# A spectral-filter and SwiGLU block: filter rows at -k turned round through DRAM, first loads reordered, nine normalisations on GpSimd

## Chip, core and metric

The kernel runs on one core of a Trainium2 chip. The metric is the device time of one execution in microseconds (us). Three runs of the kernel before gave 253.07, 253.15 and 253.79 us; their median is 253.15 us. A profile is one more execution, recorded by the hardware profiler. Its instructions span 252.6 us from the first to the last, and the execution took 254.42 us, so 1.82 us lie outside the span.

## What is computed

```
mod = (silu(c) @ w_mod).reshape(1, 6, 1, 640)
sa, ca, ga, sb, cb, gb = (mod[:, i] for i in range(6))
h = layernorm(x) * (1 + ca) + sa                       # x: 1 x 2048 x 640, bf16
y = irfft2(rfft2(h) * (w_r + 1j * w_i))                # the spectral filter
x = x + ga * y
h = layernorm(x) * (1 + cb) + sb
out = x + gb * ((silu(h @ w_gate) * (h @ w_up)) @ w_down)   # 640 -> 1728 -> 640
```

The filter `w_r`, `w_i` has 2048 rows (one for each frequency along the tokens) of 321 bf16 values (642 bytes). The kernel uses that the transform of a real signal holds a frequency k and its mirror -k together, so beside filter row k it needs row -k.

## The kernel before

**The order of the work is written out by hand.** Every engine runs its instructions in the order of the program text, with no scheduler in between. TensorE (PE), VectorE (DVE), ScalarE (ACT) and GpSimd (POOL) each have one such queue. SyncE (SP) does nothing but issue transfers, also in order. An engine that comes to a waiting instruction holds up all that stands behind it.

**The front stage** (L264 to L488) is what the change is about. The tokens are cut into eight steps `t` of two 128-token tiles each (tiles T = 2t and 2t+1):

- `bn` (L343) takes mean and variance of a tile on DVE; `bn_act` (L348) does it on ACT for the tiles in `BA` = (1, 3, 5, 11). `rstd_of` (L352) makes 1/sqrt(variance + eps), with its power on POOL (L361). `normed` (L363) writes the two normalised tiles, on DVE (L366), into one of three buffer pairs `XN`.
- `tok(t)` (L369) multiplies them by a token table `Gtab` (ten matmuls, L377) into PSUM banks 0 to 2, and ACT copies the result to `YS` (L380).
- `ddft(t)` (L382) multiplies that by `Rs`, the channel table scaled by 1 + ca (24 matmuls, L322 and L325), into PSUM banks 3 to 6, and ACT copies the result to `A_sb` (L393). For the last step, DVE and ACT share this copy (L397).
- `Rs` needs 1 + ca, which comes from `mod_cols` (L317), matmuls with the part `wm_ca` of `w_mod`. `idle_pe` (L305) are matmuls whose result nobody uses.
- `sa_cols`, `sa_rows` and `sa_fix` bring in `sa` the same way, in steps 5, 7 and after.

**The loads** (L264 to L290) stand at the top: the first two pairs of x tiles, `wm_ca`, then the rest of x between pieces of `Gtab` and the channel table `Rp`, the `sa` part of `w_mod`, a table `Ktab`, the filter rows at +k (`load_w`, L278: 128 partitions x 8 rows for each of `w_i`, `w_r`, into the slots 0 to 7 of `Wt[:, 0]` and `Wt[:, 2]`), and the first further part of `w_mod`, `wm_r[0]` (L290), which the filter stage reads at L638.

**The filter rows at -k** go to the slots 8 to 15 of the same tiles. Partition s of slot 8 + m needs row 256 m + 256 - s, and partition 0 needs row 256 m + 128. `gather` (L333) fetches one slot by an indirect load on POOL, with the row of each partition taken from `ridx`. There are 16 such loads (L336), handed out between POOL's other work by `fetch`.

**The filter stage** (L490 to L719) starts with `wsum` (L328, L331), which adds the parts of `Wt`: the columns 48 to 63 on DVE, the others on POOL. It reads all 16 slots of both, +k and -k. `prod` (L574) then multiplies the filter into the transformed data, group by group of four columns, and PE transposes and multiplies back (L551, L581, L621). `ga_mod` (L641, matmuls L638) stands on PE between the first two groups and reads `wm_r[0]` and `sc_rep`. Before, `sc_rep` is written on POOL at L669, after the front. Four transposing transfers (`t2_dma`, L502) bring the later groups, and three loads stand behind them on SP (L510 to L513).

**After that** come the inverse transform and the residual (L1152 to L1210), and the feed-forward part in four chunks (L1211 on). The change touches neither.

Of the kernel before, what the change touches and what calls it, by code (L numbers as in the profile page):

```python
# [10 lines left out]
F32 = mybir.dt.float32  # L11
# [21 lines left out]
def xslot(T):  # L33
    return NS * (T % 2) + T // 2
# [139 lines left out]
def adaln_block_kernel(ctx, tc, A_x, A_w_r, A_w_i, B_x, B_w_gate, B_w_up, B_w_down, c, w_mod, out):  # L174
# [52 lines left out]
    ridx = const.tile([P, 1], I32, name="ridx")  # L227
# [38 lines left out]
    nc.sync.dma_start(xh_sb[:, :, 0:1, :], x_v[:, :, 0:1, :])  # L266
    nc.sync.dma_start(xh_sb[:, :, 1:2, :], x_v[:, :, 1:2, :])
    nc.sync.dma_start(wm_ca[:, 0:3], wmca_v[:, 0:3])
    nc.scalar.dma_start(Rp[:, 4:5], R_dram[:, 4:5])
    nc.sync.dma_start(wm_ca[:, 3:5], wmca_v[:, 3:5])  # L270
    Gd = G_dram.rearrange("p t k f -> p t (k f)")
    nc.scalar.dma_start(Gtab[:, 0:2], Gd[:, 0:2])
    def load_x(xl, xh, gl, gh):
        nc.sync.dma_start(xh_sb[:, :, xl:xh, :], x_v[:, :, xl:xh, :])
        nc.sync.dma_start(Gtab[:, gl:gh], Gd[:, gl:gh])

    def load_w(i, w):
        nc.sync.dma_start(Wt[:, i, 0:8, 0:321], w.rearrange("(k s) l -> s k l", s=256)[0:P])  # L278

    load_x(2, 3, 2, 6)  # L280
    nc.sync.dma_start(Rp[:, 0:4], R_dram[:, 0:4])
    load_x(3, 4, 6, 8)
    load_x(4, 6, 8, 12)
    load_x(6, 8, 12, 16)
    nc.sync.dma_start(wm_sa[:], wm_v[:, :, 0:D])
    nc.sync.dma_start(Ktab[:], K_dram)
    load_w(0, A_w_i)
    load_w(2, A_w_r)
    wm_m = wm_v[:, :, 2 * D:6 * D].rearrange("p k (i d) -> p k i d", i=4)
    nc.sync.dma_start(wm_r[:, :, 0, :], wm_m[:, :, 0, :])  # L290
# [42 lines left out]
    def gather(k):  # L333
        i, m = 2 * (k // NS), k % NS
        w = (A_w_i, A_w_r)[k // NS]
        nc.gpsimd.indirect_dma_start(Wt[:, i, NS + m, 0:321], None, w, bass.IndirectOffsetOnAxis(ap=ridx[:, 0:1], axis=0),  # L336
                                     element_offset=256 * m * 321)

    if True:
        CS = (4, 0, 1, 2, 3)  # L340
        BA = (1, 3, 5, 11)

        def bn(T):  # L343
            for k in range(2):
                nc.vector.bn_stats(bn6a[:, k, :], x_sb[:, xslot(T), 320 * k:320 * k + 320])
            nc.vector.bn_aggr(mv[:, T, :], bn6a[:])
# [5 lines left out]
        def rstd_of(t):  # L352
            ts = slice(2 * t, 2 * t + 2)
            if 2 * t + 1 in BA:
                u = slice(2 * t + 1, 2 * t + 2)
                nc.vector.scalar_tensor_tensor(vtmp[:, u], mv[:, u, 0], mv[:, 2 * t + 1, 0:1], st1[:, u], ALU.mult, ALU.subtract)
                nc.vector.tensor_scalar(vtmp[:, u], vtmp[:, u], -1.0, EPS, ALU.mult, ALU.add)
                nc.vector.tensor_scalar_add(vtmp[:, 2 * t:2 * t + 1], mv[:, 2 * t, 1:2], EPS)
            else:
                nc.vector.tensor_scalar_add(vtmp[:, ts], mv[:, ts, 1], EPS)  # L360
            nc.gpsimd.tensor_tensor(rstd[:, ts], vtmp[:, ts], mhalf[:, 0:2], ALU.pow)  # L361

        def normed(t):  # L363
            for h in range(2):
                T = 2 * t + h
                nc.vector.tensor_scalar(XN[t % 3][h][:], x_sb[:, xslot(T), :], mv[:, T, 0:1], rstd[:, T:T + 1],  # L366
                                        ALU.subtract, ALU.mult)

        def tok(t, mid=()):  # L369
            Y = banks(0, 3, [6, 256])  # L370
            for s, c5 in enumerate(CS):
                if s == 3 and mid:
                    mid.pop(0)()
                for h in range(2):
                    xn = XN[t % 3][h]
                    lhsT = xn[:, 0:512].rearrange("p (m r) -> p r m", r=4)[:, c5, :] if c5 < 4 else xn[:, 512:640]
                    nc.tensor.matmul(Y[:, s, :], lhsT=lhsT, rhs=Gtab[:, 2 * t + h, :], start=(h == 0 and s % 2 == 0),  # L377
                                     stop=(h == 1 and (s % 2 == 1 or s == 4)), skip_group_check=True)
            Ys = YS[t % 3]
            nc.scalar.copy(Ys[:], Y[:, 0:5])  # L380

        def ddft(t, mid=()):  # L382
            Ys = YS[t % 3]
            for ck in range(2):
                dft_d(banks(3 + 2 * ck, 2, [4, 256]), [Ys[:, CS.index(c5), 128 * ck:128 * ck + 128] for c5 in range(NC5)])
                if mid:
                    mid.pop(0)()
            for m in mid:
                m()
            Av = A_sb[:, :, t].rearrange("p l k c r -> p k c l r")  # L390
            av = banks(3, 4, [8, 256])[:, :, 0:RC].rearrange("p (k r) (c l) -> p k c l r", k=2, c=2)
            if t < NS - 1:
                nc.scalar.copy(Av, av)  # L393
            else:
                for ls in (slice(48, 64), slice(0, 48), slice(64, 81)):
                    for ck, cp in ((0, nc.vector.tensor_copy), (1, nc.scalar.copy)):
                        cp(Av[:, ck, :, ls], av[:, ck, :, ls])  # L397

        cps = psum[:, 7, 500:500 + NC5]
# [7 lines left out]
        gathers = list(range(2 * NS))  # L407

        def fetch(n):
            for _ in range(min(n, len(gathers))):  # L410
                gather(gathers.pop(0))
# [8 lines left out]
        fetch(1)  # L420
        normed(0)
        idle_pe(4)
        mps = psum[:, 7, 0:32 * NC5]
# [9 lines left out]
        tok(0)
        for r in (1, 3):
            nc.scalar.mul(Rs[:, 0, r, :], Rp[:, r, :], one_p_ca[:, r:r + 1])
        normed(1)
        for r in range(2, 4):
            nc.gpsimd.tensor_scalar(Rs[:, 1, r, :], Rp[:, 4, :], m4c[:, r:r + 1], 1.0, ALU.mult, ALU.mult)
        for r in range(2):
            nc.vector.tensor_scalar_mul(Rs[:, 1, r, :], Rp[:, 4, :], m4c[:, r:r + 1])  # L440
        for r in (0, 2):
            nc.vector.tensor_scalar_mul(Rs[:, 0, r, :], Rp[:, r, :], one_p_ca[:, r:r + 1])
        bn(4)
        fetch(1)
        rstd_of(2)
        fetch(2)
        bn(6)
        normed(2)
        idle_pe(2)

        def sa_cols():
            mps = psum[:, 7, 431:431 + NC5]
            mod_cols(mps, wm_sa)
            nc.vector.tensor_copy(sa_col[:], mps)
            nc.gpsimd.tensor_scalar_mul(sa4[:], mask4[:], sa_col[:, 4:5])
            nc.gpsimd.tensor_copy(_rev(SL, 0, [[257, 4], [132, 2], [16, NS]]),
                                  sa_col[:, 0:4].unsqueeze(2).unsqueeze(3).to_broadcast([P, 4, 2, NS]))
            nc.gpsimd.tensor_copy(_rev(SL, 1024, [[1, 4], [132, 2], [16, NS]]),
                                  sa4[:].unsqueeze(2).unsqueeze(3).to_broadcast([P, 4, 2, NS]))

        def sa_rows():
            sps = psum[:, 7, 431:431 + NL]
            for i in range(10):
                r, c2 = i // 2, i % 2
                nc.tensor.matmul(sps, lhsT=SL[:, r, c2, :], rhs=Rp[:, r, 81 * c2:81 * c2 + 81], start=(i == 0), stop=(i == 9))
            nc.vector.tensor_scalar_mul(SAb[:], sps, 256.0)

        def sa_fix():
            fps = psum[:, 7, 431:431 + NL]
            nc.tensor.matmul(fps, lhsT=TF, rhs=SAb[:], start=True, stop=True)  # L470
            nc.vector.tensor_copy(FSA[:], fps)

        for t in range(1, NS):
            tok(t)
            if t < 6:
                (bn_act if 2 * t + 5 in BA else bn)(2 * t + 5)
                rstd_of(t + 2)
                if t < 5:
                    bn(2 * t + 6)
                normed(t + 2)  # L480
                fetch(1 + t % 2)
            ddft(t - 1)
            if t == 5:
# [11 lines left out]
    if True:  # L495
# [173 lines left out]
        nc.gpsimd.tensor_copy(sc_rep[:], sc_f[:].unsqueeze(2).to_broadcast([P, NC5, 128]))  # L669
# [640 lines left out]
```

## Time and profile before

| | us |
|---|---|
| median of three runs | 253.15 |
| the profiled execution | 254.42 |
| its span | 252.6 |
| PE busy in the span | 238.8 (95%) |
| DVE, ACT, POOL busy | 202.3, 171.1, 76.5 |
| ACT's last three copies of the front stage (L397) | 37.91 to 38.73 |
| first `wsum` on DVE starts (L331) | 39.97 |

The page of a profile has busy times by engine, the span in 40 slices of 6.3 us with a digit for the busy tenths, the transfers by queue (q1 is SP's, q10 ACT's, q0 POOL's), and the chain of work that ended last. In a line of the chain stand the start, the time and the engine with its source line. A timeline line has start, duration, engine, line, operation, output <- input and shape. `L331` is line 331 of the kernel before. A wait "for DMA" ends when a transfer has landed.

### The profile page before, as it was taken

The page shows a single profiled execution, that of the slowest core. Times are in us where ns is not written, and L with a number is a line of the kernel's source. Part 1 is how long each engine was busy: PE and PEld are TensorE (multiplying, and loading weights), DVE is VectorE, ACT ScalarE, POOL GpSimd, SP SyncE. Part 2 cuts the span into 40 slices and gives each one's busy share as a digit, 9 for nine tenths or more (in the row PEclk, how much of TensorE's full clock was granted, in tenths as well). Part 3 has the DMA queues.
Part 4 walks back from the last instruction along what each step waited for, and adds up shares of the span by engine and source line. Part 5 has one row for each costly group of instructions (what it writes and reads, how often), then busy time and mean ns, then how long its engine had stood idle before and what let it go on. Part 6 is the DMA issues. An engine that isn't in the chain of part 4 may idle for free.

```text
span 252.6 us, 5944 instructions
## 1 busy us (share of the span) xinstructions
PE 238.8 (95%) x2240; PEld 186.5 (74%) x2240; DVE 202.3 (80%) x493; ACT 171.1 (68%) x327; POOL 76.5 (30%) x111
## 2 busy tenths in 40 slices
PE   7587887999999999999999999999999999999994
PEld 2366866899989888778887778888675666656773
DVE  3695827997669999698998996778998788779964
ACT  5379876898689788858965387876247777774220
POOL 6675788671060633102001320000442000003410
PEclk9689999999999999999999999999999999999999
DMA  7999418998899999910001420300511000000111
GB/s 179 370 380 327 150 42 155 150 346 307 252 302 298 349 277 229 207 33 4 0 3 36 84 61 31 56 0 4 104 52 55 0 0 0 4 0 1 55 52 52
DMA packets 41310, 31.61 MB, mean 125 GB/s; under 512 B 22017, under 2 KB 37954, under 8 KB 41154
## 3 DMA queue, kind: packets, MB, share of 16 engines
q1 hardware_dynamic: 38704, 25.45, 36.9%
q0 software_dynamic: 2144, 5.58, 8.9%
q10 hardware_dynamic: 434, 0.21, 0.5%
q8 instruction: 17, 0.28, 0.5%
q14 instruction: 11, 0.09, 0.1%
HBM read 23.91 MB, written 2.62 MB: 105 GB/s over the span
## 4 chain that ended last, share of the span: by engine, by line
PE 83%; ACT 5%; DMA 3%; POOL 3%; DVE 2%; issue 2%; SPq 1%; DVEq 0%; ACTq 0%
PE psum L1031 35%; PE psum L902 19%; PE psum L1001 6%; PE psum L879 3%; DMA rM<-in_w_mod_dram 3%; PE psum L653 3%; PE psum L581 3%; PE psum L551 2%; PE psum L1172 2%; PE psum L1175 2%; PE psum L989 2%; POOL rW L336 2%; PE psum L377 1%; ACT rY L584 1%; PE psum L621 1%
## 5 line engine op out<-in xcount | busy, mean ns | idle before, releaser
L1031 PEld LDWEIGHTS <-rW 128*128 128x128 bf16 (+1 forms) x429 | 42.0, 98 | 12.6
L1031 PE MATMUL psum<-rW 128*128 128x256 bf16 (+1 forms) x247 | 42.2, 287 | 0.0
L928 POOL TENSOR_TENSOR rM<-rM,rL 128x320 f32<-128x320 f32 x6 | 5.4, 907 | 96.6 <-ACT rL L927 96.6
L902 PEld LDWEIGHTS <-rE 128*128 128x128 f16 (+1 forms) x196 | 19.0, 97 | 7.8
L902 PE MATMUL psum<-rE 128*128 128x320 f16 (+1 forms) x147 | 22.9, 299 | 0.0
L574 DVE TENSOR_TENSOR rM<-psum,rW 128x384 bf16<-128x384 f32 (+2 forms) x42 | 20.6, 547 | 2.1 <-PE psum L551 1.4
L1069 ACT COPY rX<-psum 128x384 f32<-128x384 f32 (+2 forms) x27 | 14.0, 519 | 7.3 <-PE psum L1031 7.2
L1062 ACT COPY rH<-psum 128x384 f32<-128x384 f32 (+2 forms) x27 | 13.9, 517 | 7.3 <-PE psum L1031 6.5
L1031 PEld LDWEIGHTS <-rE 128*128 128x128 f16 x156 | 15.2, 98 | 4.8
L1066 DVE TENSOR_TENSOR rH<-psum,rM 128x512 bf16<-128x512 f32 (+1 forms) x24 | 15.0, 624 | 4.4 <-PE psum L1031 2.6
L1085 ACT ACTIVATE rL<-psum 128x384 bf16<-128x384 f32 (+2 forms) x27 | 14.4, 532 | 5.4 <-PE psum L1031 3.4
L1070 DVE TENSOR_TENSOR rX<-psum,rX 128x384 f32<-128x384 f32 (+2 forms) x27 | 16.3, 604 | 1.7 <-ACT rX L1069 1.4
L1056 ACT COPY rM<-psum 128x384 f32<-128x384 f32 (+2 forms) x27 | 13.9, 515 | 4.0 <-PE psum L1031 3.9
L1031 PE MATMUL psum<-rE,rY 128*128 128x256 f16 (+1 forms) x78 | 15.6, 290 | 0.0
L1031 PE MATMUL psum<-rW,rE 128*128 128x256 bf16 (+1 forms) x78 | 15.6, 290 | 0.0
L1177 DVE SCALAR_TENSOR_TENSOR rM<-psum,rX 128x640 f32<-128x640 f32 x16 | 13.1, 821 | 2.7 <-ACT rL L657 1.4
L1086 ACT ACTIVATE rL<-rX 128x384 bf16<-128x384 f32 (+2 forms) x27 | 15.1, 558 | 0.0
L584 ACT CAST rY<-psum 128x512 bf16<-128x512 f32 (+2 forms) x21 | 11.8, 574 | 4.1 <-PE psum L581 3.7
L1001 PE MATMUL psum<-rW 128*128 128x256 bf16 x130 | 14.5, 273 | 0.0
L871 DVE TENSOR_TENSOR rA<-psum,rM 128x320 bf16<-128x320 f32 (+1 forms) x27 | 12.1, 472 | 2.4 <-PE psum L879 2.3
L1001 PEld LDWEIGHTS <-rW 128*128 128x128 bf16 x130 | 12.7, 98 | 1.6 <-issue 0.2
L1074 DVE TENSOR_TENSOR rH<-psum,rH 128x384 bf16<-128x384 f32 (+1 forms) x21 | 12.9, 615 | 0.0
(213 smaller groups left out, 641.7 us busy)
## 6 DMA issues: line engine op xcount, KB each, us to landing
out_dram<-rA SPq DMA_DIRECT2D x31, 80.0 KB
rM<-in_w_mod_dram SPq DMA_DIRECT2D x3, 800.0 KB
rA<-in_B_w_down_dram SPq DMA_DIRECT2D x2, 960.0 KB
rY<-in_B_w_gate_dram POOLq DMA_DIRECT2D x2, 832.0 KB
rM<-in_w_mod_dram SPq DMA_DIRECT2D x1, 1600.0 KB
rX<-in_A_x_dram SPq DMA_DIRECT2D x4, 320.0 KB
rX<-in_A_x_dram SPq DMA_DIRECT2D x2, 640.0 KB
rW<-in_B_w_gate_dram SPq DMA_DIRECT2D x2, 640.0 KB
```

Of the source, the lines that this page charges most:

```text
L574: nc.vector.tensor_tensor(PP[:, :, hl], xv[:, :, hl], in1, ALU.mult)
L584: nc.scalar.copy(Y2[:, 0:n, :], yps[:, 0:n, :])
L902: nc.tensor.matmul(o, lhsT=lhs[rows(k), k], rhs=rhs[rows(k), k], start=start and k == ks[0], stop=stop and k == ks[-1], skip_group_check=True)
L1001: nc.tensor.matmul(gu[u], lhsT=Wgu[:, u, c5, ff * 128:(ff + 1) * 128], rhs=h2T[:, :, c5, :], start=(c5 == 0), stop=(c5 == NC5 - 1))
L1031: nc.tensor.matmul(o[:, f], lhsT=w, rhs=b, start=(start and f == 0 and i == 0), stop=(stop and f == len(groups[g]) - 1 and i == len(ops) - ...
L1056: nc.scalar.copy(c0, X)
L1062: nc.scalar.copy(c2, X)
L1066: nc.vector.tensor_tensor(c11, Z, c0, ALU.add)
L1069: nc.scalar.copy(c3, X)
L1070: nc.vector.tensor_tensor(c22, Y, c3, ALU.add)
L1085: nc.scalar.activation(g21, X, ACT.Silu, scale=-1.0)
L1086: nc.scalar.activation(g22, c22, ACT.Silu, scale=-1.0)
```

## The change

The 16 indirect loads and their index `ridx` go. In their place POOL issues two transfers from DRAM to DRAM (`flip`), each of which writes 8 x 127 rows of one filter, in reversed order, to a scratch tensor. SP then loads each scratch tensor to partitions 1 to 127 (`unflip`), after a wait for its flip, and partition 0 is loaded by `edge`.

```
+    Wflip = [dram.tile([P, NS, 321], BF16, name=n) for n in ("wflip_i", "wflip_r")]
+    def edge(i, w):
+        nc.sync.dma_start(Wt[0:1, i, 8:16, 0:321], w.rearrange("(k s) l -> s k l", s=256)[P:P + 1])
+    def flip(w, f):
+        ncol = w.ap[0][0]
+        nc.gpsimd.dma_start(f[1:P].rearrange("p k l -> k p l"),
+                            bass.AP(tensor=w.tensor, offset=w.offset + 255 * ncol, ap=[[256 * ncol, NS], [-ncol, P - 1], [1, 321]]))
+    def unflip(i, f):
+        nc.sync.dma_start(Wt[1:P, i, 8:16, 0:321], f[1:P])
...
-    def gather(k):
-        i, m = 2 * (k // NS), k % NS
-        w = (A_w_i, A_w_r)[k // NS]
-        nc.gpsimd.indirect_dma_start(Wt[:, i, NS + m, 0:321], None, w, bass.IndirectOffsetOnAxis(ap=ridx[:, 0:1], axis=0),
-                                     element_offset=256 * m * 321)
```

In the built program the source of an `unflip` is 1016 rows of 321 values in one run, and its destination 127 partitions x 8 rows. A `flip` has 8 x 127 rows on both sides. An `edge` has 8 rows.

The loads on SP now stand in this order: x for steps 0 to 3 and `Gtab` for steps 0 and 1, both parts of `wm_ca`, `Rp`, the rest of `Gtab` and x in turns, the `sa` part, the filter rows at +k, the two edges, `Ktab`, then the two unflips, and `wm_r[0]` behind them. The transposing transfers follow as before.

```
+        nc.gpsimd.memset(SL[:], 0.0)
+        nc.gpsimd.tensor_copy(sc_rep[:], sc_f[:].unsqueeze(2).to_broadcast([P, NC5, 128]))
+        bn(0)
+        rstd_of(0, 0)
+        bn_act(1)
...
+        tok(0)
+        rstd_of(1)
+        bn(4)
+        normed(1)
+        rstd_of(2)
+        flip(A_w_i, Wflip[0])
+        flip(A_w_r, Wflip[1])
+        for i in range(2):
+            unflip(2 * i, Wflip[i])
+        nc.sync.dma_start(wm_r[:, :, 0, :], wm_m[:, :, 0, :])
+        tok(1)
...
+        BA = (1, 3, 5)
+        NP = {2: (0,), 3: (0,), 4: (0, 1), 5: (0, 1), 6: (0, 1), 7: (0,)}
+        def shift(t):
+            ts = slice(2 * t, 2 * t + 2)
+            nc.vector.scalar_tensor_tensor(nb1[:, ts], mv[:, ts, 0], -1.0, rstd[:, ts], ALU.mult, ALU.mult)
+        def normed_pool(t, hs):
+            for h in hs:
+                T = 2 * t + h
+                nc.gpsimd.tensor_scalar(XN[t % 3][h][:], x_sb[:, xslot(T), :], rstd[:, T:T + 1], nb1[:, T:T + 1],
+                                        ALU.mult, ALU.add)
```

`tok(0)` and `tok(1)` now stand ahead of `mod_cols` on PE, so that x and the tables are needed first and `wm_ca` later. Of the 16 normalised tiles, nine are written by POOL (the list `NP` holds 1 + 1 + 2 + 2 + 2 + 1) instead of DVE; DVE makes their offset by `shift`. Tile 11 moves from `bn_act` on ACT to `bn` on DVE. `ddft` uses PSUM banks 4 to 7 (banks 0 to 3 for its last step), and `mod_cols` bank 3. The last `YS` copy is shared by DVE and ACT. `sc_rep` is written at the start. From `t2_pe` on, the text differs only in the PSUM banks that `t2_pe` uses.

More of the change, by code (lines that the diff above doesn't have):

```diff
@@ L226, in adaln_block_kernel @@
     m4c = const.tile([P, 4], F32, name="m4c")
-    ridx = const.tile([P, 1], I32, name="ridx")
+    nb1 = const.tile([P, NT], F32, name="nb1")
     sa4 = const.tile([P, 4], F32, name="sa4")
@@ L265, in adaln_block_kernel, with load_x, load_g @@
     wmca_v = wm_v[:, :, D:2 * D]
[L266 to L270, printed above, removed]
     Gd = G_dram.rearrange("p t k f -> p t (k f)")
-    nc.scalar.dma_start(Gtab[:, 0:2], Gd[:, 0:2])
-    def load_x(xl, xh, gl, gh):
+    dram = ctx.enter_context(tc.tile_pool(name="dram", bufs=1, space=bass.MemoryType.DRAM))
+    Wflip = [dram.tile([P, NS, 321], BF16, name=n) for n in ("wflip_i", "wflip_r")]
+    def load_x(xl, xh):
         nc.sync.dma_start(xh_sb[:, :, xl:xh, :], x_v[:, :, xl:xh, :])
+    def load_g(gl, gh):
         nc.sync.dma_start(Gtab[:, gl:gh], Gd[:, gl:gh])
@@ L278, in load_w @@
         nc.sync.dma_start(Wt[:, i, 0:8, 0:321], w.rearrange("(k s) l -> s k l", s=256)[0:P])
[L280 to L284, printed above, removed]
+    def edge(i, w):
[6 more added lines that the diff above has]
+        nc.sync.dma_start(Wt[1:P, i, 8:16, 0:321], f[1:P])
+    load_x(0, 1)
+    load_x(1, 2)
+    nc.scalar.dma_start(Gtab[:, 0:2], Gd[:, 0:2])
+    load_x(2, 3)
+    load_g(2, 4)
+    load_x(3, 4)
+    nc.sync.dma_start(wm_ca[:, 0:3], wmca_v[:, 0:3])
+    nc.sync.dma_start(wm_ca[:, 3:5], wmca_v[:, 3:5])
+    nc.sync.dma_start(Rp[:], R_dram)
+    load_g(4, 8)
+    load_x(4, 6)
+    load_g(8, 12)
+    load_x(6, 8)
+    load_g(12, 16)
     nc.sync.dma_start(wm_sa[:], wm_v[:, :, 0:D])
-    nc.sync.dma_start(Ktab[:], K_dram)
     load_w(0, A_w_i)
     load_w(2, A_w_r)
+    edge(0, A_w_i)
+    edge(2, A_w_r)
+    nc.sync.dma_start(Ktab[:], K_dram)
     wm_m = wm_v[:, :, 2 * D:6 * D].rearrange("p k (i d) -> p k i d", i=4)
-    nc.sync.dma_start(wm_r[:, :, 0, :], wm_m[:, :, 0, :])
     nc.vector.memset(ones[:], 1.0)
@@ L298, in adaln_block_kernel, with idle_pe @@
                             pattern=[[-1, 128]], channel_multiplier=1)
-    nc.gpsimd.iota(ridx[:], pattern=[[0, 1]], base=256, channel_multiplier=-1)
-    nc.gpsimd.memset(ridx[0:1], 128)
     nc.scalar.activation(warm[:], warm[:], ACT.Silu)
-    def idle_pe(n, w=4):
+    def idle_pe(n, w=4, b=5):
         for i in range(n):
-            nc.tensor.matmul(banks(5, 1, [128 * w]), lhsT=ones[:], rhs=ones[:].unsqueeze(1).to_broadcast([P, w, 128]),
+            nc.tensor.matmul(banks(b, 1, [128 * w]), lhsT=ones[:], rhs=ones[:].unsqueeze(1).to_broadcast([P, w, 128]),
                              start=True, stop=True)
@@ L331, in wsum, with bn @@
         eng.tensor_tensor(v[1], v[2], v[0], ALU.add)
-    def gather(k):
-        i, m = 2 * (k // NS), k % NS
-        w = (A_w_i, A_w_r)[k // NS]
-        nc.gpsimd.indirect_dma_start(Wt[:, i, NS + m, 0:321], None, w, bass.IndirectOffsetOnAxis(ap=ridx[:, 0:1], axis=0),
-                                     element_offset=256 * m * 321)
     if True:
         CS = (4, 0, 1, 2, 3)
-        BA = (1, 3, 5, 11)
-        def bn(T):
-            for k in range(2):
+        BA = (1, 3, 5)
+        NP = {2: (0,), 3: (0,), 4: (0, 1), 5: (0, 1), 6: (0, 1), 7: (0,)}
+        def bn(T, stats=True, aggr=True):
+            for k in range(2 * stats):
                 nc.vector.bn_stats(bn6a[:, k, :], x_sb[:, xslot(T), 320 * k:320 * k + 320])
-            nc.vector.bn_aggr(mv[:, T, :], bn6a[:])
+            if aggr:
+                nc.vector.bn_aggr(mv[:, T, :], bn6a[:])
         def bn_act(T):
@@ L350, in bn_act, with rstd_of, normed @@
             nc.scalar.activation(junk1[:], x_sb[:, xslot(T), :], ACT.Identity, scale=1.0 / D, accum_out=mv[:, T, 0:1])
-        def rstd_of(t):
+        def rstd_of(t, one=None):
             ts = slice(2 * t, 2 * t + 2)
-            if 2 * t + 1 in BA:
-                u = slice(2 * t + 1, 2 * t + 2)
+            a, u = slice(2 * t, 2 * t + 1), slice(2 * t + 1, 2 * t + 2)
+            if one == 0:
+                ts = a
+            elif one == 1:
+                ts = u
+            if one != 0 and 2 * t + 1 in BA:
                 nc.vector.scalar_tensor_tensor(vtmp[:, u], mv[:, u, 0], mv[:, 2 * t + 1, 0:1], st1[:, u], ALU.mult, ALU.subtract)
                 nc.vector.tensor_scalar(vtmp[:, u], vtmp[:, u], -1.0, EPS, ALU.mult, ALU.add)
-                nc.vector.tensor_scalar_add(vtmp[:, 2 * t:2 * t + 1], mv[:, 2 * t, 1:2], EPS)
+                if one is None:
+                    nc.vector.tensor_scalar_add(vtmp[:, a], mv[:, a, 1], EPS)
             else:
                 nc.vector.tensor_scalar_add(vtmp[:, ts], mv[:, ts, 1], EPS)
-            nc.gpsimd.tensor_tensor(rstd[:, ts], vtmp[:, ts], mhalf[:, 0:2], ALU.pow)
-        def normed(t):
-            for h in range(2):
+            nc.gpsimd.tensor_tensor(rstd[:, ts], vtmp[:, ts], mhalf[:, 0:ts.stop - ts.start], ALU.pow)
+        def normed(t, hs=range(2)):
+            for h in hs:
                 T = 2 * t + h
@@ L367, in normed, with tok @@
                                         ALU.subtract, ALU.mult)
-        def tok(t, mid=()):
+        def shift(t):
+            ts = slice(2 * t, 2 * t + 2)
+            nc.vector.scalar_tensor_tensor(nb1[:, ts], mv[:, ts, 0], -1.0, rstd[:, ts], ALU.mult, ALU.mult)
+        def normed_pool(t, hs):
+            for h in hs:
+                T = 2 * t + h
+                nc.gpsimd.tensor_scalar(XN[t % 3][h][:], x_sb[:, xslot(T), :], rstd[:, T:T + 1], nb1[:, T:T + 1],
+                                        ALU.mult, ALU.add)
+        def tok(t):
             Y = banks(0, 3, [6, 256])
             for s, c5 in enumerate(CS):
-                if s == 3 and mid:
-                    mid.pop(0)()
                 for h in range(2):
@@ L378, in tok, with ddft @@
                                      stop=(h == 1 and (s % 2 == 1 or s == 4)), skip_group_check=True)
+            if t < NS - 1:
+                nc.scalar.copy(YS[t % 3][:], Y[:, 0:5])
+            else:
+                nc.vector.tensor_copy(YS[t % 3][:, 0:3], Y[:, 0:3])
+                nc.scalar.copy(YS[t % 3][:, 3:5], Y[:, 3:5])
+        def ddft(t):
             Ys = YS[t % 3]
-            nc.scalar.copy(Ys[:], Y[:, 0:5])
-        def ddft(t, mid=()):
-            Ys = YS[t % 3]
+            zb = [banks(4 + 2 * ck, 2, [4, 256]) for ck in range(2)]
+            if t == NS - 1:
+                zb = [banks(0, 2, [4, 256]), banks(2, 2, [4, 256])]
             for ck in range(2):
[L385 to L389, printed above, removed]
+                dft_d(zb[ck], [Ys[:, CS.index(c5), 128 * ck:128 * ck + 128] for c5 in range(NC5)])
             Av = A_sb[:, :, t].rearrange("p l k c r -> p k c l r")
-            av = banks(3, 4, [8, 256])[:, :, 0:RC].rearrange("p (k r) (c l) -> p k c l r", k=2, c=2)
             if t < NS - 1:
[L393 to L399, printed above, removed]
+                nc.scalar.copy(Av, banks(4, 4, [8, 256])[:, :, 0:RC].rearrange("p (k r) (c l) -> p k c l r", k=2, c=2))
+                return
+            for ls in (slice(48, 64), slice(0, 48), slice(64, 81)):
+                for ck, cp in ((0, nc.vector.tensor_copy), (1, nc.scalar.copy)):
+                    cp(Av[:, ck, :, ls], zb[ck][:, :, 0:RC].rearrange("p r (c l) -> p c l r", c=2)[:, :, ls])
+        cps = psum[:, 3, 500:500 + NC5]
         for k in range(NC5):
@@ L406, in adaln_block_kernel @@
                                 op=ALU.add)
[L407 to L411, printed above, removed]
         nc.gpsimd.memset(SL[:], 0.0)
-        fetch(2)
+        nc.gpsimd.tensor_copy(sc_rep[:], sc_f[:].unsqueeze(2).to_broadcast([P, NC5, 128]))
         bn(0)
+        rstd_of(0, 0)
         bn_act(1)
-        rstd_of(0)
-        bn(2)
-        bn_act(3)
[L420 to L423, printed above, removed]
+        bn(2, True, False)
+        rstd_of(0, 1)
+        normed(0, (0,))
+        bn(2, False, True)
+        normed(0, (1,))
+        bn_act(3)
+        bn_act(5)
+        idle_pe(6)
+        tok(0)
[9 more added lines that the diff above has]
+        tok(1)
+        idle_pe(2)
+        bn(6)
+        bn(7)
+        shift(2)
+        normed(2, [1])
+        normed_pool(2, (0,))
+        mps = psum[:, 3, 0:32 * NC5]
         mod_cols(mps, wm_ca, range(0, 3), 32)
@@ L426, in adaln_block_kernel @@
         mod_cols(mps, wm_ca, range(3, 5), 32)
-        idle_pe(3)
+        idle_pe(2)
         mps = mps.rearrange("p (c w) -> p c w", w=32)[:, :, 0]
-        rstd_of(1)
+        rstd_of(3)
         nc.vector.tensor_scalar_add(one_p_ca[:], mps, 1.0)
-        bn_act(5)
         nc.vector.tensor_scalar_mul(m4c[:], mask4[:], one_p_ca[:, 4:5])
[L433 to L439, printed above, removed]
-            nc.vector.tensor_scalar_mul(Rs[:, 1, r, :], Rp[:, 4, :], m4c[:, r:r + 1])
[L441 to L449, printed above, removed]
+        for r in range(4):
+            nc.vector.tensor_scalar_mul(Rs[:, 1, r, :], Rp[:, 4, :], m4c[:, r:r + 1])
+            if r < 2:
+                nc.vector.tensor_scalar_mul(Rs[:, 0, r, :], Rp[:, r, :], one_p_ca[:, r:r + 1])
+            else:
+                nc.scalar.mul(Rs[:, 0, r, :], Rp[:, r, :], one_p_ca[:, r:r + 1])
         def sa_cols():
-            mps = psum[:, 7, 431:431 + NC5]
+            mps = psum[:, 3, 431:431 + NC5]
             mod_cols(mps, wm_sa)
@@ L461, in sa_rows @@
         def sa_rows():
-            sps = psum[:, 7, 431:431 + NL]
+            sps = psum[:, 3, 431:431 + NL]
             for i in range(10):
@@ L468, in sa_fix @@
         def sa_fix():
-            fps = psum[:, 7, 431:431 + NL]
+            fps = psum[:, 3, 431:431 + NL]
             nc.tensor.matmul(fps, lhsT=TF, rhs=SAb[:], start=True, stop=True)
             nc.vector.tensor_copy(FSA[:], fps)
-        for t in range(1, NS):
+        for t in range(2, NS):
             tok(t)
+            if t == 2:
+                ddft(0)
+            if t < 7:
+                if t + 1 in NP:
+                    shift(t + 1)
+                normed(t + 1, [h for h in range(2) if h not in NP.get(t + 1, ())])
+                normed_pool(t + 1, NP.get(t + 1, ()))
+            for T in (2 * t + 4, 2 * t + 5):
+                if T < NT:
+                    bn(T)
             if t < 6:
-                (bn_act if 2 * t + 5 in BA else bn)(2 * t + 5)
                 rstd_of(t + 2)
[L478 to L483, printed above, removed]
+            if t == 6:
                 sa_cols()
-                fetch(16)
             if t == 7:
                 sa_rows()
-        ddft(7, [sa_fix])
+            ddft(t - 1)
+        sa_fix()
+        ddft(7)
     Em = rE.cut(0, [64, 128])
@@ L523, in t2_pe @@
             n = len(ls)
-            tp = banks((0, 1, 6, 7)[slot], 1, [8, 128], BF16)
+            tp = banks(4 + slot, 1, [8, 128], BF16)
             for i, l in enumerate(ls):
@@ L668, in adaln_block_kernel @@
         nc.gpsimd.memset(rY.cut(4096, [1600])[:], 0.0)
-        nc.gpsimd.tensor_copy(sc_rep[:], sc_f[:].unsqueeze(2).to_broadcast([P, NC5, 128]))
         t2_pe(0)
```

## The prediction

> **What bounds the kernel now.** I read the page first. PE is busy for 95% of the span and holds 83% of the chain that ended last, but the change lies in the first 40 us, so I asked for the chain, the timeline and the transfers there.
>
> ```profile
> 26.02 1.01 POOL rW L336
> 27.34 0.96 POOL rW L336
> 28.31 0.75 POOL rstd L361
> 29.08 0.81 DVE rE L366 x2
> ...
> 32.13 1.17 POOL rW L336
> 33.60 0.96 POOL rW L336
> ```
>
> This is the chain between 20 and 42 us. The reader is to see that the indirect loads stand on it: POOL computes rstd for a step only after the loads queued ahead of it, and DVE's normalisation waits. What the front hands over to is the timeline at 40 us:
>
> ```profile
> 39.97 0.43 DVE L331 TENSOR_TENSOR rW<-rW 128x512 bf16<-128x512 bf16 x1 [0.29 <-issue]
> 40.32 0.16 DVE L519 TENSOR_TENSOR rM<-psum,FSA 128x4 bf16<-128x4 f32 x1
> 40.39 0.55 DVE L331 TENSOR_TENSOR rW<-rW 128x512 bf16<-128x512 bf16 x1
> 40.54 0.32 PE L551 MATMUL psum<-Ktab,rM 128*128 128x192 bf16 x2 [0.40 <-DVE rM L519]
> 40.54 0.10 PEld L551 LDWEIGHTS <-rM 128*128 128x128 bf16 x1 [0.55 <-issue]
> 40.62 0.58 PEld L638 LDWEIGHTS <-sc_rep 128*128 128x128 bf16 x5
> 40.70 0.84 PE L638 MATMUL psum<-rM,sc_rep 128*128 128x320 bf16 x5
> ```
>
> The first wsum (L331) starts at 39.97 and waits for no transfer: every filter row is there. From its start to the end of the span are 252.6 - 39.97 = 212.6 us of work that the change leaves alone. **So the question is when wsum can start in the changed kernel**: when the front ends, or when the filter rows at -k land, whichever is later.
>
> **The rows at -k.** Removed are 16 indirect loads of 1.05 us (16.8 us of POOL) and two index instructions (0.2 us). Each had 128 rows of 642 bytes and took 2.6 to 6.2 us from issue to landing, median 4.4. Added are two flips, two edges and two unflips. An unflip moves 1016 rows of 642 bytes. What a row costs is read where the +k rows (the same shape) are loaded, at 22 to 23 us. The columns are packets, MB and the share of 16 engines' time:
>
> ```profile
> q1 hardware_dynamic: 470, 0.30, 104.8%
> ```
>
> 16 engines x 1 us x 1.048 / 470 packets = 35.7 ns for a row on one engine (over 22 to 24 us it is 37.1). I take 36. An unflip is then 1016 x 36 ns = 36.6 us of one engine's time. Spread over all 16 it would land after 2.3 us; on one engine alone after 36.6. The trace shows both ways of spreading. Over the whole span ACT's queue has this row, and up to 2 us the second one:
>
> ```profile
> q10 hardware_dynamic: 434, 0.21, 0.5%
> ```
>
> ```profile
> q10 hardware_dynamic: 2, 0.00, 1.0%
> ```
>
> ACT issues four loads or stores: c (one row) and three with 128 rows. 434 = 3 x (128 + 16) + 2, and the c load by itself is those 2: one row and one more packet, where the others have 16 more. I read the extra packets as one completion note of each engine that took part: 16 engines for an outer dimension of 128, one engine for an outer dimension of 1. A split into equal parts of the outer dimension fits both. The destination of an unflip has 127 partitions outside, and 127 has no divisor but 1 and 127: no equal split over 2 to 16 engines exists. Between the ends 2.3 and 36.6 I take 36.6, because the c row is the only one here whose outer count is not a multiple of 16, and it used one engine. Both unflips stand on SP's queue, and I count them on the same engine, one after the other: 73.2 us.
>
> [...]
>
> *When the unflips start.* The flips stand on POOL behind the power for step 2. On DVE and ACT, x lands at 4.04 as before. bn (1.10), step 0's two normalisations, bn_act of tiles 1, 3 and 5 (1.72 each, done at about 9.2), bn(4) and normed(1) bring DVE to about 10.7; the power (0.72) ends at 11.5. A flip's issue is bounded by L811's rows (0.58 us for 128 rows, 0.18 to 0.25 more for 256) and by L336 (1.05 for each 128, so 8.4); I take 0.58 + 7 x 0.2 = 2.0. Its move, in eight equal parts of the outer 8, is 127 x 36 ns = 4.6 us, plus a median landing of 4.4: the first flip lands at 22.5, the second 2 us later. The bounds are 17 (16 engines, 2.6) and 30 (issue 8.4).
>
> *Sum.* 22.5 + 0.5 (issue) + 73.2 + 1.5 (landing, from L336's smallest, 2.6, less its issue) = 97.7, about 98 us for wsum, 57.7 us later than 39.97.
>
> **What waits.** DVE's first wsum holds all DVE work behind it; POOL's own wsums (L331) wait as well; PE runs dry after stage_a(0). On SP, wm_r[0] and the four transposing transfers stand behind the unflips, and their parts on that one engine come after its rows. wm_r[0] has 640 rows of 1280 bytes, 40 of them there; such rows took 56.6 ns at 6 to 8 us (564 packets, 99.8%), so 2.3 us. L638 then starts 2.3 us after wsum instead of 0.7 and ends, 0.84 later, at 3.1, where the next group's matmuls started 2.0 us after wsum (41.98). That is +1.1. The transposed blocks come on after it, first needed 5.6 us after wsum (45.55), which covers them.
>
> *The clock.* After PE's idle stretch from 5.9 to 8.9 us the granted clock is 0.50 from 9 to 15 us. A stall of almost 60 us should bring it down again, and PE sets the pace behind wsum. Half speed for 6.8 us costs at most 3.4; I take 1.7 (0 to 3.4).
>
> **The rest of the front is worth nothing if wsum waits.** By itself: wm_ca comes behind 0.7 MB more than before, at about 11 us instead of 9.8 (at the some 370 GB/s of 8 to 14 us, 0.7 MB are 1.9 us, less what competed at 4 to 6 us), but two tok now run ahead of it. Rs is ready at about 15.7; from there ACT's copies set the pace (1.23 + 1.24 = 2.47 us a step). bn_act(11) (1.86) is gone from ACT, and the chain through POOL's loads is cut. I get the last copies at about 36.0, 2.7 us before 38.73. POOL's side: L438 (0.48 us for 162 elements) and L785 (0.61 for 256) give 1.15 for 640, so steps with two take 2.3 + 0.72 = 3.0 us against 2.5: up to 1.5 us of the gain back. The edges (8 rows each), sc_rep (0.74 us of POOL, now early), the banks and the shared copy are costed at nothing: the wait for the unflips hides all of the front. Without that wait, its gain and its POOL cost are what rival A counts.
>
> **Sum for the forecast**: 254.42 + 57.7 + 1.1 + 1.7 = 314.9, so **315 us**, against the profiled execution; the median of the runs is 1.27 lower, which is small beside the bounds. Low: flips at 17, a row at the bytes' share of the 1280-byte rows (56.6 / 2 = 28.4 ns), no extras: 17.5 + 57.7 + 1.5 = 76.7, giving 291. High: 30.5 + 2 x 1016 x 37.1 ns (75.4) + 1.5 = 107.4, with 1.1 + 3.4: 326; if the transposing transfers behind (issued from 38.58 over 7.2 us) are not covered, 334.
>
> **Rivals.**
> A. *The unflips run on several engines* and land before the front ends. For it: they hold 1016 rows, which 8 and 2 divide on the source side. Against it: 127, and the c load. Its point: 24.5 + 0.5 + 73.2/N + 1.5 below 37.3 (wsum after a front that ends at 36.0), so N of 7 or more. Time: 254.42 - 2.7 = 251.7, up to 253.2 if POOL gives 1.5 back. This is the side that is not slower. Chance 0.10.
> B. *One engine for each unflip, but not the same one.* For it: nothing in the trace tells which engine one takes. wsum at 24.5 + 0.5 + 36.6 + 1.5 = 63, time 254.42 + 23.1 + 2.8 = 280. Chance 0.03.
> C. *The flips are on one engine as well*, 36.6 instead of 4.6 us: 347. Against it is the outer 8. Chance 0.03.
> The forecast keeps 0.84.
>
> **How the numbers follow.** From 291 to 340 holds the forecast with its bounds (0.84 x 0.96 = 0.81). Two runs of this kernel can be told apart at about 0.3%. Faster by more than that (below 252.4): most of A, 0.07. Within: 0.02. Slower: 0.91.
>
> **What would show it.** In the changed kernel's profile: a stretch of some 70 us in which the share of the 16 DMA engines is about one sixteenth, at 642 bytes / 36 ns = 18 GB/s; DVE's first wsum starting near 98 with a wait for a transfer from the scratch tensors; PE nearly idle from 38 on and a granted clock of 0.5 there; SP's queue with 2 x 1016 packets of 642 bytes in that stretch. The forecast is wrong if the unflips land within some 10 us of their issue, or if wsum starts before 45. The front can be judged by itself from the last copies to A_sb: 36 to 37.5 if the second part is right.

## The result: 313.6 us against 253.4

The changed kernel took 313.6 us (median of four runs, 313.18 to 314.48), the kernel before on the same chip 253.38 us (253.07 to 253.79). The ratio is 1.238, with a 95% interval of 1.235 to 1.241. The forecast was 315 us. The profiled execution took 313.43 us with a span of 311.6.

The page of the changed kernel shows the stall in its slices of 7.8 us (PE's busy tenths, the granted clock, the busy share of the 16 DMA engines, and GB/s):

```profile
PE   7678700000004999999999999999999999999995
...
PEclk9999955555555999999999999999999999999999
DMA  7999100000029992999994000411204110000021
GB/s 190 392 239 231 48 21 21 21 21 21 21 58 193 211 400 52 323 343 293 303 190 107 3 0 2 84 55 33 45 0 87 42 44 0 0 3 1 2 77 49
```

From the sixth to the twelfth slice PE stands still, and up to the eleventh the only traffic is a steady 21 GB/s. The transfers between 34 and 36 us in the same trace (packets, MB, share of the 16 engines):

```profile
DMA packets 64, 0.04 MB, mean 21 GB/s; under 512 B 0, under 2 KB 64, under 8 KB 64
...
q1 hardware_dynamic: 64, 0.04, 7.0%
```

64 rows of 642 bytes in 2 us, one every 31 ns, at 7.0% of 16 engines (16 x 0.07 = 1.1), which is about one engine. The timeline of SP (start, how long the issue was held, line; times in us) shows who stands ahead of the unflips and behind them:

```profile
12.03 9.64 SPq L277 DMA_DIRECT2D rW<-in_A_w_r_dram  x1
21.71 6.09 SPq L280 DMA_DIRECT2D rW<-in_A_w_i_dram  x1
...
28.54 0.43 SPq L309 DMA_DIRECT2D Ktab<-tab_K  x1
29.09 0.70 SPq L288 DMA_DIRECT2D rW<-wflip_i  x1
29.90 29.59 SPq L288 DMA_DIRECT2D rW<-wflip_r  x1
59.53 31.54 SPq L458 DMA_DIRECT2D rM<-in_w_mod_dram  x1
91.19 11.24 SPq L538 DMA_TRANSPOSE rL<-rA  x3
```

L288 are the two unflips, L277 the second +k load, L280 an edge, L458 the load of `wm_r[0]`. POOL had issued the flips long before, and the profile counts 15.4 and 15.9 us from these issues to their landing:

```profile
11.52 1.34 POOL L284 DMA_DIRECT2D wflip_i<-in_A_w_i_dram  x1
12.86 1.16 POOL L284 DMA_DIRECT2D wflip_r<-in_A_w_r_dram  x1
```

And DVE's timeline, at the place of L331 in the kernel before:

```profile
96.32 0.43 DVE L349 TENSOR_TENSOR rW<-rW 128x512 bf16<-128x512 bf16 x1 [59.04 <-DMA rW<-wflip_r]
```

The first `wsum` starts at 96.32 us instead of 39.97, after waiting 59.04 us for the second unflip.

### The profile page after: what moved, and what is told of

Same layout as the page of the kernel before. It is cut to its first block, busy times and chain, and to the rows that moved or that the text cites. A ratio compares the mean times of both kernels' runs of the same rounds, so it can differ in the third digit from the quotient of the medians.

```text
span 311.6 us, 5934 instructions
## 1 busy us (share of the span) xinstructions
PE 239.1 (77%) x2241; PEld 186.6 (60%) x2241; DVE 203.8 (65%) x494; ACT 169.4 (54%) x323; POOL 69.2 (22%) x103
## 4 chain that ended last, share of the span: by engine, by line
PE 61%; DMA 17%; SPq 16%; ACT 2%; issue 1%; DVE 1%; POOL 1%; DVEq 0%; ACTq 0%
PE psum L1066 29%; PE psum L937 15%; DMA rM<-in_w_mod_dram 12%; SPq L288 10%; PE psum L1036 5%; SPq L277 3%; PE psum L914 3%; DMA rE<-tab_R 2%; DMA rW<-rL 2%; SPq L280 2%; PE psum L617 2%; PE psum L587 2%; PE psum L1024 1%; PE psum L689 1%; ACT rY L620 1%
## 5 line engine op out<-in xcount | busy, mean ns | idle before, releaser
L587 PE MATMUL psum<-Ktab,rM 128*128 128x192 bf16 x34 | 5.7, 262 | 59.3 <-DVE rM L555 59.1
L349 DVE TENSOR_TENSOR rW<-rW 128x512 bf16<-128x512 bf16 x2 | 1.0, 486 | 59.0 <-DMA rW<-wflip_r 59.0
L587 PEld LDWEIGHTS <-rM 128*128 128x128 bf16 x34 | 2.8, 102 | 60.0 <-issue 59.7
L680 ACT CAST ga_bc<-psum 128x320 bf16<-128x320 f32 x2 | 0.8, 425 | 63.0 <-PE psum L553 61.2
L349 POOL TENSOR_TENSOR rW<-rW 128x512 bf16<-128x512 bf16 (+1 forms) x10 | 10.4, 1063 | 62.1 <-DMA rW<-wflip_r 61.6
```

The costliest lines, as they stand in the source:

```text
L587: nc.tensor.matmul(xps[:, i, 0:192], lhsT=B2[:, j, :], rhs=KS2, start=True, stop=True)
```

## The experiments

The theory is the prediction's: 127 destination partitions put an unflip on one engine, both on the same one. Each run stands against the kernel before on the same chip; "wsum" is the start of DVE's first `wsum` in the profile.

### One piece of 128 partitions

```
     def edge(i, w):
-        nc.sync.dma_start(Wt[0:1, i, 8:16, 0:321], ...)
+        nc.sync.dma_start(Wflip[i // 2][0:1], ...)
     def unflip(i, f):
-        nc.sync.dma_start(Wt[1:P, i, 8:16, 0:321], f[1:P])
+        nc.sync.dma_start(Wt[:, i, 8:16, 0:321], f[:])
```

> The edge goes to row 0 of the scratch tensor (DRAM to DRAM), and one transfer loads all 128 partitions. If the count of 127 partitions put the load on one engine: 128 goes to 16 engines, 1024 rows x 31 ns / 16 = 2.0 us for each unflip, both landed by about 34 us, wsum at about 37.5 when the front ends, and the time 313.4 - 59 - 2.8 (late ga_mod and clock) = 251 to 253 us. If reading back a scratch tensor in DRAM is slow by itself: no change, wsum near 96, 313 us. If the flips or SP's order hold the load: wsum between 40 and 60, 255 to 275 us.

257.87 us, a ratio of 1.0161 (1.0142 to 1.0180). Eight rows more for each unflip take 56 us away, so the count of partitions was the cause (this edit moves the edge too; the next group leaves it where it was), and a scratch tensor in DRAM is not slow to read back. But wsum still waits for the second unflip and starts at 40.08, not 37.5:

```profile
40.08 0.43 DVE L349 TENSOR_TENSOR rW<-rW 128x512 bf16<-128x512 bf16 x1 [2.83 <-DMA rW<-wflip_r]
```

From there to the end of the span are 255.9 - 40.08 = 215.8 us, against 212.6 in the kernel before, and the time is 5 us above the upper end of what the repair was expected to give. The next groups take up both findings.

### Which count gives how many engines

```
-        nc.sync.dma_start(Wt[1:P, i, 8:16, 0:321], f[1:P])
+        nc.sync.dma_start(Wt[1:113, i, 8:16, 0:321], f[1:113])      # 122 + 5: 1:123 and 123:128
+        nc.sync.dma_start(Wt[113:128, i, 8:16, 0:321], f[113:128])
```

> Each unflip is cut into two, of 112 and of 15 partitions; the same bytes from the same rows. By the count of partitions: 112 is 16 x 7, so 896 rows x 31 / 16 = 1.7 us; 15 go to 15 engines, 8 rows x 31 = 0.25 us; wsum at about 37.5, 251 to 253 us. If the total of rows or the scratch source decides: no change, 313 us.

> Each unflip is cut into 122 and 5 partitions. By the largest divisor up to 16: 122 = 2 x 61 goes to two engines, 976 rows / 2 x 31 ns = 15.1 us each, 30.3 for both on the same two; 5 go to five engines (0.25 us). wsum at about 30 + 30.3 + 3 = 63, time 313.4 - 33 = 280 us. If only a prime count is bad and others go to 16 engines: 252. If every count that is no multiple of 16 goes to one engine: 313.

The cut at 112 gave 259.56 us (1.0222, 1.0197 to 1.0248): the same rows from the same scratch, and no stall. The cut at 122 gave 283.11 us (one run), with wsum at 65.37. The transfers of the 122 + 5 kernel between 34 and 36 us:

```profile
DMA packets 136, 0.09 MB, mean 44 GB/s; under 512 B 0, under 2 KB 136, under 8 KB 136
...
q1 hardware_dynamic: 136, 0.09, 14.0%
```

Twice the packets and twice the share of the changed kernel: two engines. In the 128-partition kernel the same two microseconds, with both unflips issued at 32.47 and 33.20, hold many more:

```profile
DMA packets 863, 0.55 MB, mean 277 GB/s; under 512 B 0, under 2 KB 863, under 8 KB 863
...
q1 hardware_dynamic: 863, 0.55, 99.2%
```

So 127 partitions went out at the share of one engine (7.0%), 122 = 2 x 61 at that of two (14.0%), 128 at that of all 16 (99.2%), and 112 without a stall (259.56 us). These counts agree with the equal split that the prediction took; the pieces of 15 and 5 were not read apart.

One detail stays open: with 112 partitions the rows took 63 ns each on average between 33 and 40 us, with 128 only 37, and wsum came at 41.63. Why was not tried.

### The same engine, whatever the queue

```
+            if i == 0:
                 unflip(2 * i, Wflip[i])
...
         ddft(7)
+        nc.scalar.dma_start(Wt[1:P, 2, 8:16, 0:321], Wflip[1][1:P])
```

> The second unflip is issued by ACT, behind its last copy of the front (about 36.5 us); the first stays on SP. If a transfer with one part always goes to the same engine, whatever queue it came by: its 1016 rows share that engine with the first, wsum near 96, 313 us as before. If each queue has its own first engine: 36.8 + 31.5 + 1.5 = 70 for wsum, 287 us.

317.05 us (one run), wsum at 100.19. While both unflips run, from 60 to 62 us, the trace has SP's queue (q1) and ACT's (q10):

```profile
DMA packets 66, 0.04 MB, mean 21 GB/s; under 512 B 0, under 2 KB 66, under 8 KB 66
...
q10 hardware_dynamic: 33, 0.02, 3.6%
q1 hardware_dynamic: 33, 0.02, 3.4%
```

Two queues, and together still 66 rows in 2 us at 3.6% + 3.4% of the 16 engines: they share one engine (16 x 0.07 = 1.1), half each. Rival B of the prediction (different engines) is out.

### What the flips cost beside others

With 128 partitions, where do the 5 us go? First, what the flips do to the loads. Transfers between 19 and 21 us, in the 128-partition kernel (q0 is POOL's queue, here the flips; q1 SP's loads):

```profile
q0 software_dynamic: 59, 0.27, 87.2%
q1 hardware_dynamic: 62, 0.08, 15.8%
```

and in the kernel before, where POOL's queue carries an indirect load:

```profile
q1 hardware_dynamic: 742, 0.57, 95.4%
q0 software_dynamic: 55, 0.11, 17.6%
```

SP's queue moves 62 packets (0.08 MB) instead of 742 (0.57 MB). The numbers of the two queues are nearly equal, and a flip's packet (0.27 MB / 59 = 4.6 KB, seven rows) holds an engine for 32 us x 0.872 / 59 = 473 ns, one of SP's for 82. The changed kernel has the same in each microsecond from 20 to 23: 31 packets of the flips to 32 of SP's, 31 to 31, 29 to 29. About one packet of SP's went out for each of the flips', and the flips' are long. So I formed the theory that later flips would land earlier things:

```
-        flip(A_w_i, Wflip[0])                 (before tok(1); with the unflips and wm_r[0] behind)
...
+            if t == 2:                        (in the loop, behind normed_pool(3))
+                flip(A_w_i, Wflip[0])         (and the rest of the same lines)
```

> The one-piece unflip of 128 partitions, with the flips issued by POOL one step later (in step 2, about 17 us instead of 11.5). Theory: from 17 to 27 us a flip's packet of seven rows goes out for each single row of SP's, so the sa weights and the +k rows crawl (SP's issue held 9.2 us), and the unflips come last, at 34 to 38.5. Issued when SP's loads are nearly through, the flips run alone: the +k rows land by about 23, the flips by 29, the unflips by 34, wsum starts at 37.5, and the time is 251 to 253 us. Rival: the total of bytes and rows before wsum is what takes till 40, whatever the order: the later flips make it later still, wsum at 43 or more, 260 us or more.

257.62 us (1.0158, 1.0113 to 1.0203), the same as with early flips, wsum at 40.53. Half of the theory held: the second +k load held SP for 3.73 us instead of 9.20. It didn't help: the flips' packets went out from 21.0 to 31.5 us instead of 16.2 to 27.2. **They go out over 10.5 to 11 us in both places** (packet by packet, the flips' 288 long ones hold the 16 engines for only 6.6 us of that with early flips and 7.5 with late ones), and the unflips' rows come behind them (34 to 39.6 us with early flips, 34.7 to 39.9 with late ones). Neither theory had the number right.

Second, the wait. An unflip of the repaired kernel waited for its edge too, which stood behind the +k rows; it was issued at 32.47, against 29.09 in the changed kernel.

```
-    load_w(0, A_w_i)
-    load_w(2, A_w_r)
     edge(0, A_w_i)
     edge(2, A_w_r)
+    load_w(0, A_w_i)
+    load_w(2, A_w_r)
```

> The one-piece unflip (257.9 us) with the two edges to the scratch tensors issued ahead of the +k rows. Theory: there the first unflip waited till 32.5 us, 3 us longer than in the changed kernel (29.1), because the edge it also waits for stood behind the +k rows; without that its rows move from 31 to 36 and land by 37.5, wsum starts at 37.5 to 38, and PE hardly idles: 252 to 254 us. Rival: the unflips' rows come behind the +k rows on the same queue whatever the wait, wsum at 39 to 40, 256 us or more.

256.22 us (1.0086, 1.0054 to 1.0118; ten runs), the time that the rival named. The unflips were issued at 29.33 and 30.07, and wsum started at 38.79, between the two expectations: 1.3 us of the 3 were the edge. The rest was the queue: in every microsecond from 28 to 38 us SP's packets kept the 16 engines at 107% or more, so the engines had no room for an earlier issue.

Third, the clock. In the 128-partition kernel PE waits 2.9 us for what stands behind `wsum` on DVE, and the windows of 2 us (PE busy, weight loads, DVE, ACT, POOL, granted clock, DMA share, GB/s) show what follows:

```profile
38.00:40.00 2.00, 0.00 (x0) 0.00 (x0) 0.00 (x0) 0.50 (x1) 0.00 (x0) 0.92 1.04 299
40.00:42.00 2.00, 0.48 (x2) 0.25 (x2) 1.80 (x5) 0.00 (x0) 1.79 (x3) 0.50 1.24 237
42.00:44.00 2.00, 1.74 (x8) 1.02 (x8) 0.36 (x2) 0.22 (x1) 1.49 (x2) 0.50 1.30 250
44.00:46.00 2.00, 1.83 (x10) 1.14 (x9) 1.16 (x4) 0.21 (x1) 0.00 (x0) 0.50 0.99 198
```

Six us at half speed. I gave PE something to do there:

```
+        idle_pe(12, 4, 1)
         PPs[0] = stage_a(0)
```

> The one-piece unflip with the early flips (257.9 us), and 12 matmuls nobody uses (some 0.21 us each at full clock, 2.6 in all) where PE idles from 37.7 to 40.6. If the half clock behind that idle stretch costs part of the 3.1 us that its filter stage lost: granted clock near 1.0 from 40 to 46 us and 255.5 to 257 us. If the late transfers alone cost it: the same time within 0.3%, or up to 0.5 us more.

256.16 us (1.0108, 1.0064 to 1.0152). The median lies where the half clock was to cost something, but the interval just overlaps that of the kernel without the matmuls, and the profiled run (257.99 us, the slowest of the four) shows no gain. There PE's wait at `wsum` is down from 2.9 to 0.5 us, but the one at L674 (`ga_mod`), which waits for `wm_r[0]`, queued on SP behind the unflips, is up from 1.1 to 1.6:

```profile
40.00:42.00 2.00, 0.79 (x6) 0.38 (x5) 1.57 (x5) 0.00 (x0) 1.45 (x3) 1.00 1.34 330
42.00:44.00 2.00, 1.07 (x5) 0.61 (x5) 0.38 (x1) 0.00 (x0) 1.84 (x2) 0.74 1.09 220
44.00:46.00 2.00, 1.83 (x11) 1.16 (x10) 0.66 (x3) 0.43 (x1) 0.00 (x0) 0.50 1.28 206
```

The clock fell 3 us later instead, and was down for about half as long. Even so, from wsum to the end of the span were 256.2 - 40.43 = 215.8 us, as without the matmuls. So in this profile the shorter slow stretch brought nothing; what the half clock costs by itself is not settled by this run. (In the first kernel under "Half of each", where `wm_r[0]` stands ahead of the unflip and the granted clock stays at 1.00, the same stretch takes 251.5 - 38.67 = 212.8 us again. Which of the two did it was not separated.)

### What the rest of the front is worth

"The one before" in the next expectation is the kernel with late flips, and this edit stands on top of it:

```
-        NP = {2: (0,), 3: (0,), 4: (0, 1), 5: (0, 1), 6: (0, 1), 7: (0,)}
+        NP = {}                               (and normed(2) whole, no shift(2))
```

> As the one before, with all normalisations back on DVE (nine tiles). If POOL's normalisations shorten the front: the last copies to A_sb end 1 us or more later than there, and the time is 0.5 to 2 us higher where wsum waits for the front. If DVE had the room all along: the same front end within 0.5 us and the same time.

256.56 us (1.0116, 1.0087 to 1.0144). ACT's last copies, first with late flips and POOL's normalisations, then with all on DVE:

```profile
35.44 0.82 ACT L425 CAST rA<-psum 128x128 bf16<-128x128 f32 x3
```

```profile
36.41 0.82 ACT L425 CAST rA<-psum 128x128 bf16<-128x128 f32 x3
```

With the nine normalisations on POOL the front is 0.97 us shorter. The time did not follow, because without them POOL issued the flips 1.9 us sooner (14.53 instead of 16.44), and wsum, which waits for the flips, came at 39.27 instead of 40.53.

The old gathers in the new front:

```
-        flip(A_w_i, Wflip[0]) ... unflip(2 * i, Wflip[i])
+        fetch(2)                              (16 indirect loads, the first two here)
...
+            fetch(2 if t < 6 else 16)         (in the loop, ahead of sa_cols; NP = {})
```

> The changed order of the loads and of the front, but with the 16 indirect loads (two a step) instead of flips and unflips, and all normalisations on DVE. If the order of the loads is what shortened the front: the last copies end at 36 to 37.5 as in the changed kernel, 251 to 252.5 us. If the indirect loads on POOL set the pace: the end of the front is at 38.5 or later, 253 to 256 us.

265.59 us (1.0479, 1.0450 to 1.0508). This one missed its question by my own placing: in step 6 six loads stood on POOL ahead of the small copies that `sa_rows` needs, and PE's longest waits are (us in total, times, longest):

```profile
PE psum L502 <- POOL rY L493: 9.0, 1, 9.0
PE psum L415 <- DVE rE L396: 2.3, 3, 1.1
```

It says nothing of the order of the loads; it shows again that a load on POOL costs what waits behind it there.

### Half of each

The rows of `w_i` by eight indirect loads, those of `w_r` by one flip and an unflip of 128 partitions (edge first, `wm_r[0]` ahead of the unflip):

```
+        flip(A_w_r, Wflip[1])
+        nc.sync.dma_start(wm_r[:, :, 0, :], wm_m[:, :, 0, :])
+        unflip(2, Wflip[1])
+        fetch(1)
...
+            if t < 6:
+                fetch(2)
```

> Half of each way: the rows at -k of the imaginary part by 8 indirect loads on POOL (two a step), those of the real part by one flip and a one-piece unflip, edge first, first part of w_mod ahead of the unflip; all normalisations on DVE. If the two flips' own 11 us of moving are what keeps wsum at 40: one flip ends by 23, the unflip lands by 34, wsum waits for the front alone (last copies 36.4 as with late flips and DVE, wsum 37.5 to 38), 251 to 252.5 us, faster than before. If the 8 loads on POOL slow the steps: front at 38 or later, 253 us or more.

> As the one before, with seven normalisations on POOL, one a step and two in one (the changed kernel has nine). POOL then has 0.7 + 0.9 + 2 x 1.26 = 4.1 us a step against DVE's 3.4: if POOL sets the pace, the front ends later than with all on DVE and the time is 0.5 to 2 us higher; if only some steps have two loads and the slack covers them, it ends up to 0.7 us earlier, 250.5 to 252 us.

All on DVE: 254.27 us (1.0031, 1.0011 to 1.0051), a little slower than before. wsum no longer waits for any transfer, as expected, but starts at 38.67 behind a front that ends at 37.4. With seven normalisations on POOL: 258.09 us (1.0154, 1.0116 to 1.0193), worse than expected; PE waited 5.0 us for them (four times), and wsum started at 43.41. POOL has room here for the loads or for the normalisations, not for both.

In the first of the two, DVE's timeline has this in each of four steps:

```profile
22.46 0.17 DVE L389 TENSOR_SCALAR vtmp<-mv 128x2 f32<-128x2 f32 x1
23.47 0.80 DVE L395 TENSOR_SCALAR rE<-rX,mv,rstd 128x640 bf16<-128x640 bf16 x2 [0.84 <-POOL rstd L390]
```

DVE asks POOL for rstd and has nothing to do until it comes. The kernel before puts the next tile's statistics there; the changed front had lost that. So, last:

```
-            (normed of step t + 1, then bn(2 * t + 4) and bn(2 * t + 5))
+            if t == 2:
+                normed(3)
+                bn(8)
             if t < 6:
+                bn(2 * t + 5)
                 rstd_of(t + 2)
+                if t < 5:
+                    bn(2 * t + 6)
+                normed(t + 2)
```

> The half-and-half version (254.3 us) with one change of order on DVE: the statistics of one further tile stand between asking POOL for rstd and the normalisation that waits for it, as in the kernel before, where there DVE waited 0.81 to 0.85 us in each of four steps. If that wait is what set its step of 4.05 us: the step falls to POOL's 0.7 + 2 x 1.26 = 3.2 us, the last copies end 2 to 3 us earlier (34.4 to 35.4 instead of 37.4), wsum starts at 36 to 37, and the time is 251.3 to 252.5 us, faster than before. If wsum then waits for the late indirect loads or the unflip: wsum at 38 or later and 253.5 to 254.5 us.

252.65 us (twelve runs), a ratio of 0.9938 (0.9908 to 0.9969): **0.6% faster than the kernel before**. POOL's timeline has one rstd every 3.2 us, as worked out, instead of 4.05:

```profile
19.91 0.70 POOL L390 TENSOR_TENSOR rstd<-vtmp,mhalf 128x2 f32<-128x2 f32 x1 [4.64 <-DVE vtmp L389]
...
23.11 0.74 POOL L390 TENSOR_TENSOR rstd<-vtmp,mhalf 128x2 f32<-128x2 f32 x1
...
26.31 0.74 POOL L390 TENSOR_TENSOR rstd<-vtmp,mhalf 128x2 f32<-128x2 f32 x1
```

The last copies end at 36.0 and wsum starts here, after 0.33 us of issue and no transfer:

```profile
37.30 0.43 DVE L351 TENSOR_TENSOR rW<-rW 128x512 bf16<-128x512 bf16 x1 [0.33 <-issue]
```

All three come a little later than expected (34.4 to 35.4, 36 to 37, and 252.5 us at most). The span is 250.8 us, 1.8 less than before, though wsum starts 2.67 us sooner: DVE's second `wsum` took 1.46 us instead of 0.55, for a reason that was not tried. It was not tried either whether the new order on DVE would do as much with all sixteen indirect loads, without any flip.

## Why the prediction was right, point by point

- *127 means one engine, and the same one twice.* Shown: 64 rows in 2 us with 127 (7.0% of 16 engines), 136 with 122 (14.0%), 863 with 128 (99.2%), and 66 by two queues together (7.0%). The c load, one row and one more packet where the loads of 128 rows have 16 more, had pointed the right way.
- *A row takes 36 ns on that engine.* Mis-sized: 31 to 32. The busy time of a row's packet is 34 to 35 ns also when nothing else runs, as at 22 to 23 us before (35.7), but one row follows another every 31, so that busy time per packet was the wrong measure of the rate. From the first issue to wsum less its landing, 2032 rows took 94.8 - 29.6 = 65.2 us instead of 73.2.
- *The flips land at 22.5.* Mis-sized the other way, though within its bounds (17 to 30). They were issued as assumed (11.52 and 12.86, 1.34 and 1.16 us, against 2.0 each), but landed 15.4 and 15.9 us after that instead of 11, at 26.9 and 28.8. I had priced the move by rows from DRAM to SBUF on free engines (4.6 us); from DRAM to DRAM, behind x and the tables and packet for packet with SP's loads, both flips took 11 us. SP came to the first unflip only at 29.09, because the +k load and an edge had held it 9.64 and 6.09 us; I had not counted that at all. The two errors, +6.6 for the start and -8.0 for the rows, nearly cancel: 96.32 against 97.7. The mechanism was right; that the sum came this close was luck.
- *What waits, and the clock.* From wsum to the end of the span were 311.6 - 96.32 = 215.3 us, against 212.6 before: +2.7, and 1.1 + 1.7 = 2.8 forecast. `ga_mod` started 1.87 us after wsum (2.3 forecast), its five matmuls took 1.49 us instead of 0.84, and the granted clock was 0.50 in the windows from 50 to 100 us and 0.91 from 100 to 110. PE has no wait for the transposed blocks there: they were covered. How the 2.7 us split between the late `ga_mod` and the clock was not measured.
- *The front by itself.* ACT's last copies ended at 36.33 instead of 38.73: 2.4 us earlier, 2.7 forecast. POOL's normalisation took 0.87 to 0.94 us, not 1.15, and where the prediction had it cost up to 1.5 us of the front's gain, the front with late flips was 0.97 us shorter with it than without.
- *Rival A was priced wrong.* The prediction had it at 251.7 to 253.2 us with 7 or more engines; with 128 partitions the time is 257.9. Two terms failed: the unflips' landing (40 us, not about 31), for the reasons just given, and the idle PE with the late `wm_r[0]` and the half clock (215.8 us from wsum to the end, where I counted 212.6). Had the count been 128, the forecast would have missed by 5 us.

## What to carry to other kernels

Count the outer dimension of each transfer before its bytes: the rows of both unflips went out in under 6 us with 128 partitions and took 65 with 127, on one engine, and a second queue didn't add an engine. Where one partition is special, let it be part of the tile (128) and mend it elsewhere. And a transfer that is off every engine's program isn't free: these flips went out over 11 us in which the loads beside them crawled (from 19 to 21 us they moved 0.08 MB in the 128-partition kernel, 0.57 in the kernel before), while the sixteen indirect loads that they replaced cost POOL 16.8 us, but no engine waited for their data at wsum. The better version takes half of each and fills DVE's wait for rstd.

## What the runs showed of the hardware

- An SP issue was held for 30 us behind a transfer on one engine: L288 for 29.59 and L458 for 31.54 us, each about one unflip long, without waiting for any semaphore that the trace names.
- DRAM to DRAM in seven-row packets of 4494 bytes (q0, 128-partition kernel): 473 ns each between 19 and 21 us and 364 on average over the 288 of both flips, 52 to 68 ns for a row where one from DRAM to SBUF takes 31 to 36.
- An idle stretch of PE of 2.9 us came with about 6 us at a granted clock of 0.50 (40 to 46 us, 128-partition kernel). With the added matmuls two waits of 0.5 and 1.6 us, close together, came with some 3 us of it. After 59 us without work the half clock lasted until about 5 us after PE's work came back (96.88).
